# Start of a fused sparse-attention and MoE kernel: one load on another queue, mask copies dealt out anew, one subtraction on another engine

## The chip, the cores and the metric

One core of one Trainium2 chip runs the whole program. The time is device microseconds of one execution, and each kernel is given by the median of several runs. A profiled execution gives the trace; its span goes from the first to the last instruction, and the execution around it is a little longer.

## What is computed

Block-sparse attention over 4 batches of 8 heads (768 positions, 64 channels), and a two-layer feed-forward network on its output. Everything is float32 and has to come out at nearly float32 accuracy.

```python
scores = scale * np.matmul(q, k.transpose(0, 1, 3, 2))
mask = np.abs(blk_i - blk_j) <= window            # blocks of 32 positions, window 1
mask = mask | (blk_i == 0) | (blk_j == 0) | (blk_i == n_blocks - 1) | (blk_j == n_blocks - 1)
for qb in range(n_blocks):
    for kb in sampled_blocks[qb]:                 # 3 sampled blocks for each block row
        mask[qb * block:(qb + 1) * block, kb * block:(kb + 1) * block] = True
scores = np.where(mask, scores, -1000000000.0)
attn = np.exp(scores - np.max(scores, axis=-1, keepdims=True))
attn = attn / (np.sum(attn, axis=-1, keepdims=True) + 1e-09)
out = np.matmul(attn, v)
# then: h = x @ w_in; g = piecewise(h); return g @ w_out
```

## The kernel before

A float32 product is made of float32r products. A value is split into a high part (its value rounded to float32r) and a low part (the value less the high part). For a head, `load_qk` (L214) brings 64 rows of q and 64 rows of k, transposed, into one 128x768 tile `qk`; `hi` (L218, recorded at the helper's L196) rounds it on ScalarE into `qkh`; `lo` (L228) subtracts, on VectorE, and leaves the low part in the tile `qk`. Transfers from SBUF to SBUF then deal the rows out: `hi_one` (L224, L225) writes `KA` and `QA`, `hi_two` (L233, L234) writes the high halves of `QB` and `KB`, and `lo_two` (L237, L238) their low halves. They all go through SyncE's queue (SP), as nearly every transfer of the kernel does.

`KA` and `QA` are 128-row operands in which the rows above 64 carry the mask. Rows 64 and up of `KA` hold indicator rows (which block a column belongs to) and a row of ones for each query tile; rows 64 to 87 of `QA` hold the mask's penalties, and rows 96 and up the negated row maxima. So one matmul gives masked scores. There are two sets of these operands (`SETS = 2`): even heads use `QA[0]` and `KA[0]`, odd heads `QA[1]` and `KA[1]`.

The first computation of a head is twelve matmuls `max_mm` (L267), high part only, each followed by a maximum on VectorE (`max_red`, L272). The maxima are turned by a transpose with the identity `idr` (L280) and written to `QA` (L283). Then come the scores (L303 with `KA` and `QA`, L304 with `KB` and `QB`), the exponentials on ScalarE (L308) and the product with v (L333). Heads 0 to 9 use a simpler product with v. Beside the heads, the weights arrive as 64-bit numbers and are turned into float32 high and low parts (`convert`, L157 to L184: ScalarE L168, VectorE L169 to L174, ScalarE L196, GpSimd L180), and the two layers of the network follow batch by batch (L457 to L459, L485 to L487).

`consts` (L87 to L124) prepares the masks once. It loads the sampled blocks, a table, the indicator rows `ind` (38 rows of 768 numbers, into a borrowed buffer `raw`, L100) and the identity (L102). VectorE rounds the identity into `idr` (L103) and the indicator rows into `KA[0]` (L104); GpSimd rounds them into `KA[1]` (L108, recorded at L194). VectorE builds a 24x24 penalty table `mb`. For each half of the columns (384 of them) one matmul (L122) multiplies it with the indicator rows of `KA[0]` into one bank of PSUM, and the result is copied into rows 64 to 87 of both sets of `QA` (L124): set 0 by VectorE, set 1 by ScalarE.

The steps are put into a list with a planned time each and sorted by it; the plan of `consts` is at -90, the first `load_qk` at -99, the other steps of head 0 between -13 and 0. The framework's scheduler takes that order as a priority and not as a fixed order: on each engine it puts what it thinks is ready first. The order in the trace is the one that it made. It also gives the transfers from SyncE's and ScalarE's queues eight completion semaphores, in turn.

Of the kernel before, what the change touches and what calls it, by code (L numbers as in the profile page):

```python
# [10 lines left out]
I32 = mybir.dt.int32  # L11
U32 = mybir.dt.uint32
AF = mybir.ActivationFunctionType
ALU = mybir.AluOpType
# [4 lines left out]
B, H, S, D = 4, 8, 768, 64  # L19
NB, BLK, NR = 24, 32, 3  # L20
T = 6
HALF = 384
# [5 lines left out]
KM = 64 + NB  # L28
KA = 96 + T
# [8 lines left out]
def body(ctx, tc, qk_t, v, sampled_blocks, moe_w_in, moe_w_out, ind, cm, negd, ident, fold, out):  # L38
    nc = tc.nc
# [11 lines left out]
    op = pool("op", 1)  # L51
    wst = pool("wst", 3)
    cv = pool("cv", 1)
# [19 lines left out]
    def f(ap):  # L73
        return ap.bitcast(F32)


    idr = cst.tile([128, 128], F32R, name="idr")
# [4 lines left out]
    QA = [cst.tile([128, S], F32R, name=f"QA{i}") for i in range(SETS)]  # L82
# [4 lines left out]
    def consts():  # L87
        M = slice(64, KM)
        for i in range(SETS):
            nc.gpsimd.memset(f(QA[i][64:128 if i == 0 else 96]), 0.0)  # L90
        nc.gpsimd.memset(VW[0][:, :, 64:128], 1.0)
        nc.gpsimd.memset(VW[1][:, :, 0:64], 1.0)
        nc.vector.memset(eps, 1e-9)
        nc.vector.memset(half_c, 0.5)
        sraw = cst.tile([128, NR, 2], I32, name="sraw")
        nc.sync.dma_start(out=sraw[M], in_=sampled_blocks.bitcast(I32).rearrange("a (r w) -> a r w", w=2))
        cmt = cst.tile([128, 2 * NB], F32, name="cmt")
        nc.sync.dma_start(out=cmt[M], in_=cm)
        ef = f(cv.tile([128, 512, 2], I32, name="raw", bufs=3).rearrange("p c w -> p (c w)"))[64:KA, 0:S]
        nc.sync.dma_start(out=ef, in_=ind)  # L100
        idf = pp.tile([128, HALF], F32, name="pt")[:, 0:128]
        nc.sync.dma_start(out=idf, in_=ident)  # L102
        nc.vector.tensor_copy(out=idr, in_=idf)  # L103
        nc.vector.tensor_copy(out=KAt[0][64:KA], in_=ef)  # L104
        nc.sync.dma_start(out=nd, in_=negd.rearrange("a (t p) -> a t p", t=T))
        nc.sync.dma_start(out=sel, in_=fold)
        for i in range(1, SETS):
            rounded(nc.gpsimd, KAt[i][64:KA], ef)  # L108
        sf = cst.tile([128, NR], F32, name="sf")
        nc.vector.tensor_copy(out=sf[M], in_=sraw[M, :, 0])  # L110
        al = cst.tile([128, NB], F32, name="al")
        nc.vector.tensor_copy(out=al[M], in_=cmt[M, 0:NB])
        for r in range(NR):
            nc.vector.scalar_tensor_tensor(
                out=al[M], in0=cmt[M, NB:2 * NB], scalar=sf[M, r:r + 1], in1=al[M],
                op0=ALU.is_equal, op1=ALU.max)
        mb = cst.tile([128, NB], F32R, name="mb")
        nc.vector.tensor_scalar(out=mb[M], in0=al[M], scalar1=-1.0, scalar2=BIG, op0=ALU.add, op1=ALU.mult)
        for hf in range(2):
            cs = slice(hf * HALF, (hf + 1) * HALF)  # L120
            pm = psa.tile([128, 512], F32, name="pa")
            nc.tensor.matmul(out=pm[0:NB, 0:HALF], lhsT=mb[M], rhs=KAt[0][64:KM, cs], start=True, stop=True)  # L122
            for i in range(SETS):
                (nc.scalar.copy if i else nc.vector.tensor_copy)(out=QA[i][64:KM, cs], in_=pm[0:NB, 0:HALF])  # L124


    plan = []
# [62 lines left out]
    def rounded(eng, dst, src):  # L190
        if eng is nc.vector:
            eng.tensor_copy(out=dst, in_=src)
        elif eng is nc.gpsimd:
            eng.tensor_scalar(out=dst, in0=src, scalar1=1.0, scalar2=0.0, op0=ALU.mult, op1=ALU.add)  # L194
        else:
            eng.copy(out=dst, in_=src)  # L196

    def head(i, n0, b, h, pst):
# [7 lines left out]
        st = {}  # L206
# [18 lines left out]
            move(QAi[0:64], st["hi"][L])  # L225

        def lo():
            nc.vector.tensor_tensor(out=st["x"], in0=st["x"], in1=f(st["hi"]), op=ALU.subtract)  # L228

        def hi_two():  # L230
            st["KB"] = qk.tile([128, S], F32R, name="KB")
# [8 lines left out]
        def split(pl, n, src, hi, lo):  # L240
            t = st[n] = pl.tile([128, T, 128], F32R, name="vn")
            rounded(nc.scalar, t[:, :, hi], st[src])
            nc.gpsimd.tensor_tensor(out=t[:, :, lo], in0=st[src], in1=f(t[:, :, hi]), op=ALU.subtract)
# [12 lines left out]
        at(pre - G["qs"] - 0.4, hi)  # L256
        at(pre - G["qs"] + 0.2, hi_one)
        at(pre - G["qs"] + 0.4, lo)
        at(pre - G["qs"] + 1.3, hi_two)
        at(pre - G["qs"] + 1.6, lo_two)  # L260
# [21 lines left out]
        def max_row(lo=0, n=T):  # L282
            nc.vector.tensor_tensor(out=QAi[96:96 + n].rearrange("a (t p) -> a t p", t=T)[:, lo:n],  # L283
                                    in0=st["pr"][0:n, 0:128].unsqueeze(1).to_broadcast([n, n - lo, 128]),
                                    in1=nd[0:n, lo:n], op=ALU.mult)
# [240 lines left out]


    at(TC, consts)
    for i in range(NHEADS):
        b, h = divmod(i, H)  # L530
# [4 lines left out]
    p = PER * H / (2 * NF)  # L535
# [3 lines left out]
    for fq in range(4):  # L539
        for kt in range(4):  # L540
            cs = slice(fq * 512, (fq + 1) * 512)
# [86 lines left out]
```

## Time and profile before

| | us |
|---|---|
| median of 3 runs | 993.7 |
| the runs | 993.34, 993.7, 997.28 |
| the profiled execution | 991.61 |
| its span | 989.8 |
| busy in it: TensorE matmuls | 947.2 (96%) |
| VectorE | 735.9 (74%) |
| ScalarE | 637.2 (64%) |
| GpSimd | 323.5 (33%) |

PE is TensorE, PEld its weight loads, DVE VectorE, ACT ScalarE, POOL GpSimd, SP SyncE. A "q" behind an engine's name (SPq) means its sequencer, which issues transfers. In a timeline the first two columns are the start and the time, in us; behind a row stands the idle time of the engine before it and what ended it. A busy PE is not PE at its peak, since matmuls overlap: in a packed stretch they follow one another sooner than each one's own time.

### The profile page before, as it was taken

The page shows a single profiled execution, that of the slowest core. Times are in us where ns is not written, and L with a number is a line of the kernel's source. Part 1 is how long each engine was busy: PE and PEld are TensorE (multiplying, and loading weights), DVE is VectorE, ACT ScalarE, POOL GpSimd, SP SyncE. Part 2 cuts the span into 40 slices and gives each one's busy share as a digit, 9 for nine tenths or more (in the row PEclk, how much of TensorE's full clock was granted, in tenths as well). Part 3 has the DMA queues.
Part 4 walks back from the last instruction along what each step waited for, and adds up shares of the span by engine and source line. Part 5 has one row for each costly group of instructions (what it writes and reads, how often), then busy time and mean ns, then how long its engine had stood idle before and what let it go on. Part 6 is the DMA issues. An engine that isn't in the chain of part 4 may idle for free.

```text
span 989.8 us, 14583 instructions
## 1 busy us (share of the span) xinstructions
PE 947.2 (96%) x4687; PEld 830.4 (84%) x4687; DVE 735.9 (74%) x1349; ACT 637.2 (64%) x1302; POOL 323.5 (33%) x283
## 2 busy tenths in 40 slices
PE   5898899999899999999999999999999999999998
PEld 3666567778779989999989999998999899899996
DVE  5888887679998887888888897888888885422222
ACT  3676666666667666777767676866777676533433
POOL 1222120225554344444544444344544444000000
PEclk9999999999999999999999999999999999999999
DMA  6666676753455454656455454655546442434442
GB/s 196 200 182 184 190 207 204 228 180 103 155 170 172 128 141 129 186 151 174 136 143 175 133 150 137 184 158 152 156 130 187 116 124 86 154 128 128 160 128 96
DMA packets 56216, 154.43 MB, mean 156 GB/s; under 512 B 9612, under 2 KB 17952, under 8 KB 56140
## 3 DMA queue, kind: packets, MB, share of 16 engines
q1 hardware_dynamic: 56100, 153.48, 52.1%
q8 instruction: 37, 0.61, 0.3%
q14 instruction: 39, 0.32, 0.1%
q10 hardware_dynamic: 40, 0.03, 0.0%
HBM read 100.92 MB, written 14.81 MB: 117 GB/s over the span
## 4 chain that ended last, share of the span: by engine, by line
PE 70%; DVE 7%; ACT 2%; issue 1%; POOL 0%; POOLq 0%; ACTq 0%; DVEq 0%
PE oa L485 8%; PE oa L487 8%; PE oa L486 8%; PE hp L457 7%; PE hp L458 7%; PE hp L459 7%; PE po L335 5%; PE pa L303 4%; PE pa L304 4%; PE po L336 4%; PE pa L267 4%; DVE pl L316 2%; DVE mc L272 1%; PE pa L459 1%; PE pa L458 1%
## 5 line engine op out<-in xcount | busy, mean ns | idle before, releaser
L323 POOL TENSOR_TENSOR acc<-acc,pt 128x384 f32<-128x384 f32 x176 | 206.6, 1174 | 189.9 <-ACT pt L308 146.2
L272 DVE TENSOR_REDUCE mc<-pa 128x1 f32<-128x384 f32 x384 | 203.3, 549 | 20.4 <-PE pa L267 17.1
L196 ACT CAST ph<-pt 128x384 fp32r<-128x384 f32 x264 | 135.8, 514 | 94.4 <-PE po L335 90.1
L316 DVE TENSOR_TENSOR pl<-pt,ph 128x384 fp32r<-128x384 f32 x264 | 166.9, 632 | 33.3 <-ACT ph L196 32.4
L308 ACT ACTIVATE pt<-pa 128x384 f32<-128x384 f32 x288 | 140.5, 489 | 49.6 <-PE pa L304 41.6
L457 PE MATMUL hp<-x,wi 128*128 128x384 f32 x448 | 156.3, 349 | 5.4 <-DVE r L469 5.3
L485 PE MATMUL oa<-w,gh 128*128 128x512 f32 x384 | 153.3, 399 | 0.3 <-ACT gh L196 0.3
L459 PE MATMUL hp<-x,wi 128*128 128x384 f32 x448 | 152.1, 340 | 0.0
L458 PE MATMUL hp<-x,wi 128*128 128x384 f32 x448 | 152.0, 339 | 0.0
L487 PE MATMUL oa<-w,gl 128*128 128x512 f32 x384 | 151.5, 394 | 0.0
L486 PE MATMUL oa<-w,gh 128*128 128x512 f32 x384 | 150.8, 393 | 0.0
L267 PE MATMUL pa<-KA,QA 88*128 88x384 f32 x384 | 139.4, 382 | 8.8 <-DMA QA<-qkh 5.9
L469 DVE SCALAR_TENSOR_TENSOR r<-r,hp 128x384 f32<-128x384 f32 x112 | 61.8, 552 | 74.6 <-ACT r L466 74.4
L478 DVE TENSOR_TENSOR gl<-r,gh 128x384 fp32r<-128x384 f32 x128 | 91.0, 711 | 30.2 <-ACT gh L196 28.1
L267 PEld LDWEIGHTS pa<-KA,QA 88*128 88x128 f32 x384 | 73.4, 193 | 33.2 <-DVE mc L272 11.2
L303 PE MATMUL pa<-QA,KA 102*128 102x384 f32 x288 | 99.7, 346 | 0.7 <-DVE mc L272 0.4
L463 ACT ACTIVATE r<-hp,half_c 128x384 f32<-128x384 f32 x112 | 65.1, 581 | 52.3 <-PE hp L459 49.2
L304 PE MATMUL pa<-QB,KB 128*128 128x384 f32 x288 | 98.3, 341 | 0.0
L335 PE MATMUL po<-ph,vn 128*128 128x384 f32 x264 | 91.9, 348 | 4.7 <-DVE xun L345 3.9
L457 PEld LDWEIGHTS hp<-x,wi 128*128 128x128 f32 x448 | 85.0, 190 | 12.3 <-DVE r L469 7.8
L323 POOL TENSOR_TENSOR acc<-pt 128x384 f32<-128x384 f32 x44 | 45.6, 1037 | 136.7 <-ACT pt L308 132.9
L336 PE MATMUL po<-pl,vn 128*128 128x384 f32 x264 | 88.8, 336 | 0.0
(97 smaller groups left out, 1665.7 us busy)
## 6 DMA issues: line engine op xcount, KB each, us to landing
w<-wo_dram SPq DMA_DIRECT2D x112, 512.0 KB
qk<-in_qk_t_dram SPq DMA_DIRECT2D x32, 384.0 KB
raw<-in_moe_w_in_dram SPq DMA_DIRECT2D x16, 512.0 KB
raw<-in_moe_w_out_dram SPq DMA_DIRECT2D x16, 512.0 KB
wo_dram<-w SPq DMA_DIRECT2D x16, 512.0 KB
lv<-in_v_dram SPq DMA_DIRECT2D x32, 192.0 KB
KA<-qkh SPq DMA_DIRECT2D x32, 192.0 KB
QA<-qkh SPq DMA_DIRECT2D x32, 192.0 KB
```

The costliest lines, as they stand in the source:

```text
L267: nc.tensor.matmul(out=pm[:, 0:HALF], lhsT=QAi[0:KM, t * 128:(t + 1) * 128], rhs=KAi[0:KM, kh * HALF:(kh + 1) * HALF], start=True, stop=True)
L272: nc.vector.reduce_max(out=st["mc"][:, t, kh:kh + 1], in_=st.pop(("pm", t, kh))[:, 0:HALF], axis=AX.X)
L308: nc.scalar.activation(out=p, in_=st.pop(("ps", c))[:, 0:HALF], func=AF.Exp, scale=SCALE)
L316: (nc.gpsimd if i < 2 * H and c in PL1 else nc.vector).tensor_tensor(out=pl, in0=st["p", c], in1=f(st["ph", c]), op=ALU.subtract)
L323: nc.gpsimd.tensor_tensor(out=st["acc", hf], in0=prev, in1=st["p", c], op=ALU.add)
L335: nc.tensor.matmul(out=po, lhsT=st["vn"][:, c], rhs=st["ph", c], start=(c == 0), stop=False)
L457: nc.tensor.matmul(out=hv, lhsT=wi[:, j, 0, fs], rhs=x[:, 0], start=(j == 0), stop=False)
L458: nc.tensor.matmul(out=hv, lhsT=wi[:, j, 0, fs], rhs=x[:, 1], start=False, stop=False)
L459: nc.tensor.matmul(out=hv, lhsT=wi[:, j, 1, fs], rhs=x[:, 0], start=False, stop=(j == NP - 1))
L485: nc.tensor.matmul(out=o, lhsT=gh[:, ts], rhs=w[:, 0], start=(fi == 0), stop=False)
L486: nc.tensor.matmul(out=o, lhsT=gh[:, ts], rhs=w[:, 1], start=False, stop=False)
L487: nc.tensor.matmul(out=o, lhsT=gl[:, ts], rhs=w[:, 0], start=False, stop=(fi == NF - 1))
```

## The change

Three edits in `consts` and one in `head`. The load of the indicator rows is issued from ScalarE's queue, and written ahead of the other loads of `consts`. The identity is rounded by ScalarE, as the last statement of `consts`, instead of by VectorE. The copies of the mask rows are dealt out by half instead of by set: VectorE copies the first half of the columns into both sets, ScalarE the second half. And `lo` of head 0 (`i` is the number of the head) is done by GpSimd instead of VectorE; every other head keeps it on VectorE.

```diff
         nc.vector.memset(half_c, 0.5)
+        ef = f(cv.tile([128, 512, 2], I32, name="raw", bufs=3).rearrange("p c w -> p (c w)"))[64:KA, 0:S]
+        nc.scalar.dma_start(out=ef, in_=ind)
         sraw = cst.tile([128, NR, 2], I32, name="sraw")
         nc.sync.dma_start(out=sraw[M], in_=sampled_blocks.bitcast(I32).rearrange("a (r w) -> a r w", w=2))
         cmt = cst.tile([128, 2 * NB], F32, name="cmt")
         nc.sync.dma_start(out=cmt[M], in_=cm)
-        ef = f(cv.tile([128, 512, 2], I32, name="raw", bufs=3).rearrange("p c w -> p (c w)"))[64:KA, 0:S]
-        nc.sync.dma_start(out=ef, in_=ind)
         idf = pp.tile([128, HALF], F32, name="pt")[:, 0:128]
         nc.sync.dma_start(out=idf, in_=ident)
-        nc.vector.tensor_copy(out=idr, in_=idf)
         nc.vector.tensor_copy(out=KAt[0][64:KA], in_=ef)
...
             for i in range(SETS):
-                (nc.scalar.copy if i else nc.vector.tensor_copy)(out=QA[i][64:KM, cs], in_=pm[0:NB, 0:HALF])
+                (nc.scalar.copy if hf else nc.vector.tensor_copy)(out=QA[i][64:KM, cs], in_=pm[0:NB, 0:HALF])
+        nc.scalar.copy(out=idr, in_=idf)
...
         def lo():
-            nc.vector.tensor_tensor(out=st["x"], in0=st["x"], in1=f(st["hi"]), op=ALU.subtract)
+            (nc.vector if i else nc.gpsimd).tensor_tensor(out=st["x"], in0=st["x"], in1=f(st["hi"]), op=ALU.subtract)
```

## Rows read from the trace of the kernel before

**Rows 1.** The page: the busy time of each engine, and PE's busy share in 40 equal slices of the span (a digit is a slice's share in tenths).

```profile
PE 947.2 (96%) x4687; PEld 830.4 (84%) x4687; DVE 735.9 (74%) x1349; ACT 637.2 (64%) x1302; POOL 323.5 (33%) x283
...
PE   5898899999899999999999999999999999999998
```

**Rows 2.** Busy time of the engines by stretch (the stretch, its length, then PE, PEld, DVE, ACT, POOL in us with the count of instructions, the granted clock, the DMA share and GB/s).

```profile
0.00:25.00 25.00, 13.55 (x41) 9.75 (x42) 14.47 (x35) 9.23 (x17) 3.50 (x9) 1.00 0.68 196
25.00:50.00 25.00, 22.38 (x89) 16.57 (x88) 22.06 (x42) 15.72 (x32) 6.24 (x4) 0.93 0.67 197
50.00:100.00 50.00, 45.27 (x186) 32.08 (x184) 43.41 (x82) 35.80 (x73) 10.45 (x8) 1.00 0.68 186
100.00:150.00 50.00, 43.67 (x173) 29.88 (x172) 43.97 (x84) 33.88 (x69) 9.53 (x7) 1.00 0.69 199
150.00:200.00 50.00, 49.17 (x223) 39.03 (x223) 34.88 (x67) 30.55 (x61) 6.13 (x5) 1.00 0.67 212
200.00:250.00 50.00, 46.19 (x217) 39.34 (x216) 40.95 (x70) 33.58 (x68) 19.40 (x16) 0.97 0.45 136
250.00:300.00 50.00, 45.25 (x217) 38.37 (x216) 48.47 (x81) 33.55 (x72) 27.06 (x22) 0.97 0.51 163
...
600.00:800.00 200.00, 198.72 (x1047) 182.89 (x1048) 167.24 (x306) 142.21 (x296) 89.27 (x80) 1.00 0.53 154
```

**Rows 3.** The timeline of the first 20 us, all engines and the queues (rows between them left out).

```profile
0.74 1.28 ACT L196 ACT_TABLE_LOAD   x1 [0.74 <-PEq L608]
0.74 0.40 SPq L214 DMA_DIRECT2D qk<-in_qk_t_dram  x1
...
2.02 0.26 SPq L100 DMA_DIRECT2D raw<-in_ind_dram  x1
...
4.03 0.83 ACT L196 CAST qkh<-qk 128x768 fp32r<-128x768 f32 x1 [2.00 <-DMA qk<-in_qk_t_dram]
...
4.88 0.53 SPq L221 DMA_DIRECT2D KA<-qkh  x1
...
5.46 0.59 SPq L221 DMA_DIRECT2D QA<-qkh  x1
...
7.61 0.46 SPq L221 DMA_DIRECT2D KB<-qkh  x1
7.61 0.56 DVE L104 CAST KA<-raw 38x768 fp32r<-38x768 f32 x1 [2.35 <-DMA raw<-in_ind_dram]
7.76 1.10 POOL L194 TENSOR_SCALAR KA<-raw 38x768 fp32r<-38x768 f32 x1 [4.78 <-DMA raw<-in_ind_dram]
8.20 1.47 DVE L228 TENSOR_TENSOR qk<-qk,qkh 128x768 f32<-128x768 f32 x1
...
8.23 0.83 PE L122 MATMUL pa<-KA,mb 24*24 24x384 f32 x2 [8.23 <-DVE KA L104]
9.59 0.21 DVE L103 CAST idr<-pt 128x128 fp32r<-128x128 f32 x1
...
9.84 1.01 DVE L124 CAST QA<-pa 24x384 fp32r<-24x384 f32 x2
10.20 0.60 SPq L238 DMA_DIRECT2D KB<-qk  x1
10.48 0.87 ACT L124 CAST QA<-pa 24x384 fp32r<-24x384 f32 x2 [5.62 <-DVE QA L124]
...
11.36 2.93 PE L267 MATMUL pa<-KA,QA 88*128 88x384 f32 x6 [2.31 <-DMA QA<-qkh]
...
13.76 0.33 SPq L214 DMA_DIRECT2D qk<-in_qk_t_dram  x1
...
15.19 0.27 PE L280 MATMUL pa<-idr,mr 128*3 128x128 f32 x1 [0.90 <-DVE mr L276]
...
16.91 0.52 PE L304 MATMUL oa<-QB,KB 128*128 128x384 f32 x1
...
19.77 0.66 ACT L168 ACTIVATE cva<-raw 128x512 f32<-128x512 f32 x1
```

**Rows 4.** What SyncE's queue waited for in the first 30 us, and the transfer that TensorE's first score matmul waited for in the same stretch (us in total, times, longest).

```profile
SPq L214 <- DMA KB<-qk: 1.0, 1, 1.0
...
SPq L221 <- DMA raw<-in_ind_dram: 0.9, 1, 0.9
...
PE pa L267 <- DMA QA<-qkh: 2.3, 1, 2.3
```

**Rows 5.** Half-microsecond stretches of the start, columns as in rows 2; the last two are the busy share of the 16 DMA engines and GB/s.

```profile
2.50:3.00 0.50, 0.00 (x0) 0.00 (x0) 0.00 (x0) 0.00 (x0) 0.49 (x2) 1.00 0.85 338
...
5.50:6.00 0.50, 0.00 (x0) 0.00 (x0) 0.00 (x0) 0.00 (x0) 0.00 (x0) 1.00 0.18 65
...
9.00:9.50 0.50, 0.06 (x1) 0.00 (x0) 0.50 (x1) 0.00 (x0) 0.00 (x0) 1.00 0.98 209
...
10.00:10.50 0.50, 0.00 (x0) 0.00 (x0) 0.50 (x2) 0.02 (x1) 0.00 (x0) 1.00 0.14 31
```

**Rows 6.** GpSimd's groups of subtractions and additions by shape (count, then busy us and mean ns, then the idle time before them), and all of VectorE's `lo` (shortest, median and longest ns, first and last start).

```profile
L323 POOL TENSOR_TENSOR acc<-pt 128x384 f32<-128x384 f32 x44 | 45.6, 1037 | 136.7 <-ACT pt L308 132.9 <-DVE psum L358 3.8
...
L180 POOL TENSOR_TENSOR w<-cva,w 128x512 fp32r<-128x512 f32 x16 | 22.7, 1420 | 74.8 <-DVE gl L478 37.3 <-ACT w L196 32.8 <-DMA QA<-qkh 4.7
...
L228 DVE TENSOR_TENSOR qk<-qk,qkh x32: 893/946/1466, 8.2 to 779.5; 128x768 f32<-128x768 f32 x32
```

## The prediction

> **What bounds the kernel now.** I read the page first: TensorE is busy for 947.2 of 989.8 us, and the only slice far below the others is the first, at five tenths [rows 1]. The change touches nothing but that slice, so I then read the busy time by stretch: the first 25 us hold 13.55 us of matmuls; later stretches are packed to 99% (198.72 of 200) or, between 25 and 300 us, to 87 to 98%, with VectorE at 70 to 97% beside them [rows 2]. The reader is to see that there is no second place where the edits act directly: what they can give is the time by which the first score matmul starts earlier, passed on to a kernel that is mostly TensorE from then on.
>
> Next the timeline of the start, read backwards from that matmul. L267 starts at 11.36, and what released it is the transfer into `QA` [rows 3, 4]. That transfer was issued at 5.46, so it took 5.9 us [rows 3]. The mask path, which the change mostly rebuilds, was done a little earlier: indicator rows landed by 7.61, `KA` copy to 8.17, mask matmuls to 9.06, then VectorE did `lo` (8.20 to 9.67) and `idr` before it got to its mask copies at 9.84, which ended at 10.85 [rows 3]. So there are two paths into the first matmul, and the mask copies of set 0 are the second to last, half a microsecond ahead of `QA`. Ending that path earlier gives nothing unless `QA` also lands earlier.
>
> Why is `QA` so slow? While it is still under way, at 10.0 to 10.5, the DMA engines are busy for 0.14, some two of sixteen; at 9.0 to 9.5 they were at 0.98 [rows 5]. The same picture stands at 5.5 to 6.0 (0.18, 65 GB/s), when the indicator rows are what is outstanding [rows 3, 5]. I read this as two engines that carry the whole of `ind` and fall behind with their shares of everything queued after it, `KA` and `QA` among them.
>
> **The load of the indicator rows.** Before, it is the fourth transfer on SyncE's queue, issued at 2.02 and landed at 7.61: 5.6 us [rows 3]. ScalarE issues nothing in this stretch. An issue there costs between 0.26 and 0.60, as SyncE's do, and with the table load of 1.28 it ends long before `qk` releases ScalarE at 4.03 (idle 2.00 before it) [rows 3], so the issue itself is hidden. Issued at 0.74 with the same 5.6 us, `ind` lands at 6.3. The bounds: as quick as `qk` on all engines, 3.3 us, gives 4.0; if the table load goes first on ScalarE, it is issued near 2.0 and lands at 7.6, as now [rows 3]. I take 6.3, since the row is the same transfer. In return `qk` may be later: at 338 GB/s [rows 5] one of 16 engines moves 21 GB/s, its share of the 384 KB is 24 KB or 1.1 us, and if it alternates with `ind` on two engines, `qk` lands up to 1.1 us later.
>
> **The wait that comes with it.** The issue of `KB` at 7.61 waited for `ind`, though it doesn't read it [rows 3, 4]. Transfers take eight completion semaphores in turn: `ind` was the fourth and `KB` the twelfth. With `ind` moved to first or second place, its follower eight places on is `KA` or `QA`. So one of the two now waits for `ind` to land. Behind the waiting issue stand, in SyncE's queue, the other moves, `lo_two`, the next v, the first raw weights and the next `qk`. `QA` is issued at 6.4 if it is the one that waits, or at 6.9 behind `KA`, whose issue takes 0.53 [rows 3], instead of 5.46. A delay of `hi` by 1.1 us (end at 6.0, `KA` at 6.05) is covered by that wait to within 0.3 us.
>
> How long does `QA` take then? With `ind` landed, the two engines are free of it. The nearest row without that backlog is `KB<-qk`, issued at 10.20 and landed when it releases the next `qk` at 13.76: 3.56 us [rows 3, 4]. That gives 9.96 or 10.5; the middle is 10.2, **1.2 us earlier** than 11.36. The bounds: `ind` at 4.0 leaves `QA` at its old 5.46 and 9.0, so -2.3; the old 5.9 us from the new issue gives 12.3 or 12.8, so +0.9 to +1.4. I stay near the first price, because the tail at two engines [rows 5] is gone once `ind` is through.
>
> **The mask path** after: `ind` at 6.3, `KA` copy 0.56, mask matmuls 0.83, then two copies on each engine side by side, 1.01 on VectorE and 0.87 on ScalarE [rows 3]: 8.7. Before, ScalarE's copies of a half waited for VectorE's of the same half; that wait goes. The path is 1.5 us ahead of `QA` and gives nothing by itself; if that cover went, it would still allow 8.7.
>
> **`idr` on ScalarE**: one small copy, 0.21 on VectorE [rows 3], up to the 0.44 of a mask copy on ScalarE. Its reader is the transpose at 15.19, some 4 us later even after a shift of 1.2. Nothing.
>
> **`lo` on GpSimd.** GpSimd takes 1037 ns for 384 columns and 1420 for 512 [rows 6], so 2.1 us for 768, against 1.47 here and 0.95 usually on VectorE [rows 6]. It needs `hi` and, if the scheduler keeps the written order, stands behind GpSimd's `KA[1]` copy of 1.10, which waits for `ind`: 6.3 + 1.1 + 2.1 = 9.5, against 9.67 before. With `ind` at 7.6 it is 10.8. Its moves feed L304 at 16.91, and the second one landed at 13.76: 3.1 us of cover. The raw weights behind them in SyncE's queue are first read at 19.77 [rows 3]. Nothing, up to a delay of 3 us.
>
> **The sum**: -1.2 us at the first matmul. The maxima, the transpose and the first scores hang on it step by step [rows 3], so I carry the whole of it to the end: 989.8 becomes 988.6, and 991.61 becomes 990.4. The profiled execution lies 2.1 below the median of 993.7, and two of three runs are within 0.4 of that, so I subtract from the median: **992.5**.
>
> **The rivals.** *The two engines stay the last.* Both queues may be served by the same engines, so the two slow ones carry the same bytes before `QA`'s, whatever the queue; `QA` lands at 11.3 as now. For it: the tail of two engines is what ends last [rows 5]. Against it: `ind` is issued 1.3 us sooner (0.74 for 2.02), and if the two engines start on it sooner, they are through with the list sooner. The time is 993.7. The Trainium skill (DMA: Bandwidth & Descriptors, section Issuing engines are not separate DMA queues) states just this: transfers from several engines interleave on the same 16 DMA engines, and another issuing engine saves only the time to issue. By that rule the gain is near nothing; no row of this stretch has two queues at work, so the trace can't decide it.
>
> *`QA` hangs on `ind`* and loses. The place is the semaphore wait on SyncE; the price is the new issue time plus the old 5.9 us, +0.9 to +1.4, so 994.9. It decides against the change from the point at which `ind` lands later than 7.7, or 7.2 with `KA` in front (11.36 less 3.56, less the issue). For it: the wait is seen today on `KB` [rows 4]; against it: `ind` must become slower than it is.
>
> *The scheduler's order changes further on.* The trace shows that it doesn't keep the written order: L103 runs after L228, which is written much later [rows 3]. A start with other times can turn pairs on VectorE and ScalarE for a long stretch. What that can move is TensorE's idle time from 25 to 300 us: 2.6 + 4.7 + 6.3 + 0.8 + 3.8 + 4.8 = 23 us [rows 2]. A quarter of it either way is 6 us: 988 or 999.
>
> **How the numbers follow.** Chances: the forecast 0.50, the two engines 0.15, the semaphore 0.13, another order 0.22, half to each side, of which 0.09 and 0.11 reach beyond 0.5%. That is 5.0 us, about what a measurement of this kernel can tell from no change; its own runs spread over 4. So faster 0.09, same 0.80, slower 0.11. The range takes in -2.3, +1.4, the spread of the runs above the median (997.28), and the smaller part of the reorderings: 988.8 to 997.5.
>
> **What would show it.** Right: L267 starts near 10.2, released by a transfer into `QA` or `KA`; SyncE waits for `ind` at `KA` or `QA` and no longer at `KB`; the two-engine tail before L267 is gone. Wrong: L267 still at 11.3 (two engines), later than 11.4 (semaphore), or a start that moved while TensorE's busy share between 25 and 300 us changed by more than the shift (order). A mask copy as the releaser of L267 would show that I priced the `QA` transfer too high.

## The result, and the profile after

The changed kernel took 998.87 us (median of 8 runs, 997.85 to 1002.19) beside 993.03 for the kernel before (8 runs, 989.69 to 997.28): a ratio of 1.0063, with an interval of 1.0043 to 1.0083. It is slower, by some 6 us, where the prediction said 1.2 us faster; the time lies above its range.

The page of the changed kernel, as [rows 1]: the same work, more idle time, and the first slice down from five tenths to three.

```profile
span 997.4 us, 14588 instructions
...
PE 950.7 (95%) x4687; PEld 832.6 (83%) x4687; DVE 735.3 (74%) x1347; ACT 637.6 (64%) x1303; POOL 325.1 (33%) x284
...
PE   3898889998899999999999999999999999999998
```

Busy time by stretch, as [rows 2]. TensorE does 9.89 us of matmuls in the first 25, where it did 13.55, a lack of 3.7, and another 1.0 less in the next 25. Between 600 and 800 it is as packed as before (199.03 of 200 us).

```profile
0.00:25.00 25.00, 9.89 (x28) 7.31 (x29) 14.53 (x32) 8.38 (x15) 6.59 (x11) 1.00 0.72 194
25.00:50.00 25.00, 21.38 (x75) 14.81 (x74) 22.93 (x39) 15.77 (x32) 5.73 (x5) 0.86 0.68 188
...
600.00:800.00 200.00, 199.03 (x1047) 183.19 (x1047) 166.01 (x305) 142.43 (x297) 87.44 (x78) 1.00 0.52 153
```

The timeline of its start, as [rows 3] (line numbers from L96 to L123 are one or two off those of before).

```profile
0.74 0.55 ACTq L96 DMA_DIRECT2D raw<-in_ind_dram  x1
0.74 0.39 SPq L214 DMA_DIRECT2D qk<-in_qk_t_dram  x1
...
5.91 0.83 ACT L196 CAST qkh<-qk 128x768 fp32r<-128x768 f32 x1 [3.31 <-DMA qk<-in_qk_t_dram]
6.61 0.33 SPq L162 DMA_DIRECT2D raw<-in_moe_w_in_dram  x1
6.62 0.56 DVE L103 CAST KA<-raw 38x768 fp32r<-38x768 f32 x1 [5.72 <-DMA raw<-in_ind_dram]
...
7.05 0.53 SPq L221 DMA_DIRECT2D KA<-qkh  x1
...
7.63 0.59 SPq L221 DMA_DIRECT2D QA<-qkh  x1
...
7.95 1.80 POOL L228 TENSOR_TENSOR qk<-qk,qkh 128x768 f32<-128x768 f32 x1
7.99 2.34 DVE L113 SCALAR_TENSOR_TENSOR al<-cmt,sf,al 24x24 f32<-24x24 f32 x3
...
10.59 0.83 PE L121 MATMUL pa<-KA,mb 24*24 24x384 f32 x2 [10.59 <-DVE mb L117]
...
11.21 1.01 DVE L123 CAST QA<-pa 24x384 fp32r<-24x384 f32 x2 [0.68 <-PE pa L121]
...
13.94 0.43 DVE L170 TENSOR_SCALAR cva<-cva 128x512 int32<-128x512 int32 x1
...
14.14 1.30 PE L267 MATMUL pa<-KA,QA 88*128 88x384 f32 x3 [2.72 <-DMA QA<-qkh]
14.40 0.69 DVE L172 SCALAR_TENSOR_TENSOR cva<-raw,cva 128x512 int32<-128x512 int32 x1
15.13 0.69 DVE L174 SCALAR_TENSOR_TENSOR cva<-raw,cva 128x512 int32<-128x512 int32 x1
15.74 2.87 DVE L272 TENSOR_REDUCE mc<-pa 128x1 f32<-128x384 f32 x6
...
18.86 0.27 PE L280 MATMUL pa<-idr,mr 128*3 128x128 f32 x1 [0.90 <-DVE mr L276]
```

Four things are to be seen. The indicator rows came 1.0 us earlier (6.62 for 7.61), but q and k 1.9 later (5.91 for 4.03). In SyncE's queue a load of 512 KB of raw weights now stands ahead of `KA` and `QA`; before, the first such load was issued after all of head 0's moves. `QA` was issued at 7.63 and releases L267 at 14.14: 6.5 us, beside 5.9 before. The traces also hold the times at which a transfer's completion semaphore rose, sixteen times for `QA`: before, fourteen of these rises had come by 9.14 and the last two came at 10.90 and 11.23, the tail that the prediction put down to two engines; here all sixteen came between 11.95 and 14.00. That tail is gone, and the whole of `QA` is late. And when the first score matmul was done, VectorE was busy with the weights' conversion (L170 to L174), so the first maximum (L272) waited until 15.74. The first transpose (L280), which was at 15.19, is at 18.86: the start is 3.7 us late.

What SyncE's queue waited for in the first 20 us (us in total, times, longest): the weight load, not `KA` or `QA`, is now the transfer eight places behind `ind`.

```profile
SPq L162 <- DMA raw<-in_ind_dram: 2.9, 1, 2.9
```

### The profile page after: what moved, and what is told of

It reads as the page before. It is cut to its first block, busy times and chain, and to the rows that moved or that the text cites. A ratio compares the mean times of both kernels' runs of the same rounds, so it can differ in the third digit from the quotient of the medians.

```text
span 997.4 us, 14588 instructions
## 1 busy us (share of the span) xinstructions
PE 950.7 (95%) x4687; PEld 832.6 (83%) x4687; DVE 735.3 (74%) x1347; ACT 637.6 (64%) x1303; POOL 325.1 (33%) x284
## 4 chain that ended last, share of the span: by engine, by line
PE 78%; DVE 12%; ACT 3%; issue 3%; DMA 3%; POOL 1%; SPq 0%; ACTq 0%; DVEq 0%; POOLq 0%
PE oa L485 8%; PE oa L487 8%; PE oa L486 8%; PE hp L457 7%; PE hp L459 7%; PE hp L458 7%; PE pa L267 6%; PE po L335 5%; PE pa L303 5%; PE pa L304 4%; PE po L336 4%; DVE mc L272 3%; PE po L333 3%; PE oa L333 2%; DVE pl L316 2%
## 5 line engine op out<-in xcount | busy, mean ns | idle before, releaser
L272 DVE TENSOR_REDUCE mc<-pa 128x1 f32<-128x384 f32 x384 | 203.2, 548 | 24.3 <-PE pa L267 21.2
L267 PE MATMUL pa<-KA,QA 88*128 88x384 f32 x384 | 139.4, 382 | 9.1 <-DVE mc L272 4.5
L267 PEld LDWEIGHTS pa<-KA,QA 88*128 88x128 f32 x384 | 73.9, 194 | 32.6 <-DVE mc L272 12.1
L304 PE MATMUL pa<-QB,KB 128*128 128x384 f32 x288 | 98.1, 340 | 0.0
```

Source lines behind the costliest of these rows:

```text
L267: nc.tensor.matmul(out=pm[:, 0:HALF], lhsT=QAi[0:KM, t * 128:(t + 1) * 128], rhs=KAi[0:KM, kh * HALF:(kh + 1) * HALF], start=True, stop=True)
L272: nc.vector.reduce_max(out=st["mc"][:, t, kh:kh + 1], in_=st.pop(("pm", t, kh))[:, 0:HALF], axis=AX.X)
```

## The experiments

The column "L280" is the start of the first transpose in the profiled execution (15.19 before; the line is L283 in the kernels with added lines); it tells how late the start is. All times are medians beside runs of the kernel before on the same chip (993.03 for the changed kernel, 992.91 for the next four rows, 992.2 for the four after them, 993.63 for the last three). The ratio and its interval are an estimate of their own and not the quotient of the two medians (e_hold: 1.0023, where the medians give 1.0005).

| run | L280, us | shift | median, us | ratio to before (interval) |
|---|---|---|---|---|
| the changed kernel | 18.86 | +3.67 | 998.87 | 1.0063 (1.0043 to 1.0083) |
| e_queue | 18.39 | +3.20 | 1000.57 | 1.0083 (1.0055 to 1.0111) |
| e_noqueue | 14.90 | -0.29 | 993.95 | 1.0012 (0.9993 to 1.0031) |
| e_spread | 12.61 | -2.58 | 988.83 | 0.9957 (0.9938 to 0.9976) |
| e_aspread | 17.47 | +2.28 | 996.73 | 1.0046 (1.0028 to 1.0064) |
| e_hold | 15.51 | +0.32 | 992.7 | 1.0023 (1.0004 to 1.0043) |
| e_hold_nolo | 14.44 | -0.75 | 989.88 | 0.9979 (0.9958 to 0.9999) |
| e_slow | 16.40 | +1.21 | 991.46 | 0.9996 (0.9979 to 1.0014) |
| e_spread_nq | 13.47 | -1.72 | 989.2 | 0.9977 (0.9959 to 0.9994) |
| e_wfirst | 18.93 | +3.74 | 1000.33 | 1.0061 (1.0037 to 1.0085) |
| e_mended | 13.60 | -1.59 | 990.16 | 0.9961 (0.9945 to 0.9978) |
| e_spread_copies | 12.58 | -2.61 | 991.05 | 0.9971 (0.9949 to 0.9994) |

### Which of the edits

e_queue is the kernel before with the first edit alone; e_noqueue is the changed kernel without it.

```diff
 # e_queue, against the kernel before
+        ef = ... [64:KA, 0:S]
+        nc.scalar.dma_start(out=ef, in_=ind)
         sraw = cst.tile([128, NR, 2], I32, name="sraw")
...
-        nc.sync.dma_start(out=ef, in_=ind)
 # e_noqueue, against the changed kernel: the same lines the other way round
```

> The kernel before with one edit alone: the indicator rows issued from ScalarE's queue, ahead of the other loads. Theory Q (the queue edit is the whole loss): like the changed kernel, 5 to 6.5 us over before; SyncE sends the first raw weights ahead of KA and QA, head 0's q and k land near 5.9 instead of 4.0, the first score matmul L267 starts at 13.5 to 14.2. Rival G (the subtraction on GpSimd is the loss, since it triples VectorE's three small steps on the penalty table and delays the mask matmul from 8.2 to 10.6): within 1 us of before.

> The changed kernel with the indicator rows back on SyncE's queue in their old place; the mask copies by half, the identity on ScalarE and the subtraction on GpSimd stay. Theory Q: within 1 us of before (-1 to +0.5), L267 at 11.3 since QA still lands there, the mask copies end near 9.3 to 10. Rival G: 4 to 6 us over before.

Theory Q held in both: the queue edit alone gives the whole loss, and without it the time is that of before within the interval. The sizes are off (7.7 us between the medians for a forecast of 5 to 6.5, and 1.0 for at most 0.5). The other edits are not the cause. The mask copies by half did what they should (in e_noqueue L267 was released by `QA` at 11.07, 0.9 us after the last mask copy), and it bought nothing, as forecast. In e_queue the whole order of TensorE's work is that of the changed kernel, and SyncE sends the weights first (6.52, then `KA` at 6.96); in e_noqueue the orders of TensorE and SyncE are those of before. So the order of the work follows the queue edit.

### Is the weight load the cause, or ScalarE's queue?

e_hold keeps all of the change and holds back the first two weight loads; e_wfirst keeps the kernel before and sends the first weight load early.

```diff
 # e_hold, against the changed kernel, in convert's load()
             st["raw"] = cv.tile([128, 512, 2], I32, name="raw", bufs=3)
+            loads.append(1)
+            if len(loads) <= 2:
+                nc.gpsimd.tensor_copy(out=f(st["raw"])[0:64, 0, 0:1], in_=f(QA[0])[0:64, 0:1])
 # e_wfirst, against the kernel before, in plan_conversions(); n counts the conversions from the last planned
-            at(t - P["cl"], load)
+            at(-12.6 if n == len(conv) - 1 else t - P["cl"], load)
```

> The changed kernel, in which the first two loads of raw weights wait until QA of head 0 has landed (GpSimd copies one column of QA into each raw tile before its load; the tile is then overwritten). Theory W (the weight load that SyncE sends ahead of KA and QA, and the conversion steps that then stand ahead of the maxima, are half of the late start): QA lands near 11 instead of 14, L267 starts at 11 to 12.5, the first column of maxima is 0.5 to 1.5 us later than before instead of 3.7, and the end 1 to 2 us over before. Rival O (the new order further on costs by itself): the first maxima as said, but the end still 3 us or more over before.

> The kernel before with one thing changed: the first load of raw weights is planned right after head 0's rounding, so that SyncE sends it ahead of KA and QA. The indicator rows stay on SyncE, the mask copies, the identity and the subtraction stay as before. From there on every engine's order is that of the changed kernel. Theory W (that weight load is the cause, by its traffic ahead of QA and its conversion steps ahead of the maxima): L267 at 13 to 14.5, the first maxima 3 to 4 us late, the end 4.5 to 6.5 us over before, as in the changed kernel. Rival Q2 (ScalarE's queue itself is the cause, since q and k come 1.9 us later there): less than 3 us over before.

The timeline of e_wfirst. `ind` is on SyncE's queue as before, q and k land as early as before, the mask copies end at 11.3, and still L267 starts at 14.28 behind `QA`, which was issued at 5.30.

```profile
3.87 0.83 ACT L196 CAST qkh<-qk 128x768 fp32r<-128x768 f32 x1 [1.85 <-DMA qk<-in_qk_t_dram]
3.95 0.42 SPq L162 DMA_DIRECT2D raw<-in_moe_w_in_dram  x1
...
5.30 0.59 SPq L221 DMA_DIRECT2D QA<-qkh  x1
...
10.28 1.01 DVE L124 CAST QA<-pa 24x384 fp32r<-24x384 f32 x2
...
14.28 1.30 PE L267 MATMUL pa<-KA,QA 88*128 88x384 f32 x3 [4.78 <-DMA QA<-qkh]
```

Theory W held from both sides. With the loads held back, the change costs 0.3 us at the start and 1.0023 (0.4 to 4.3 us by the interval, 0.5 between the medians); with nothing but the early weight load, the kernel before is as slow as the changed one (1.0061 beside 1.0063) and late by the same 3.7 us. That q and k land 1.9 us later on account of ScalarE's queue is real, and alone it costs little: e_hold has it too (rounding at 5.80). There `QA` was issued at 7.24 and had landed by 10.40, when GpSimd's copy of its column starts: 3.2 us, and earlier than in the kernel before. The mask copies were the last into the first score matmul.

```profile
7.24 0.59 SPq L224 DMA_DIRECT2D QA<-qkh  x1
...
10.40 0.30 POOL L164 COPY raw<-QA 64x1 f32<-64x1 f32 x2 [0.80 <-DMA QA<-qkh]
...
11.66 2.96 PE L270 MATMUL pa<-KA,QA 88*128 88x384 f32 x6 [0.40 <-DVE QA L123]
```

The two runs don't weigh the same. Holding the loads also gave TensorE an order of its own: it differs from that of before up to matmul 483 and from that of the changed kernel up to 617, so e_hold is not the changed kernel less one transfer. In e_queue and e_wfirst TensorE's order is that of the changed kernel in all 4687 matmuls, and these two carry the argument. What the changed order costs further on, apart from the load's traffic, no run separates.

Why the load came forward was not tried; it was read from the program. The scheduler fills a queue with whatever it thinks ready. Before, SyncE still had loads to issue when it took head 0's rounding to be done; with one load fewer there was a gap, and the next ready transfer, planned much later, went into it.

### Two DMA engines

e_spread and e_slow are the kernel before with the indicator rows in two transfers; the order of work on every engine is that of before, but for one pair: VectorE does head 0's subtraction ahead of the `KA` copy and not behind it. e_aspread is the changed kernel with 32 and 6 rows.

```diff
-        nc.sync.dma_start(out=ef, in_=ind)
 # e_spread (e_aspread: the same on nc.scalar)
+        [nc.sync.dma_start(out=ef[r0:r1], in_=ind[r0:r1]) for r0, r1 in ((0, 32), (32, 38))]
 # e_slow
+        [nc.sync.dma_start(out=ef[r0:r1], in_=ind[r0:r1]) for r0, r1 in ((0, 37), (37, 38))]
```

> The kernel before with the indicator rows loaded by two transfers on SyncE's queue, of 32 and 6 rows, instead of one of 38; every engine's order of work is that of before. If one transfer of 38 rows is carried by two DMA engines and these hold up QA (the reading of the prediction), QA lands near 9, the indicator rows near 5, L267 starts at 9 to 10, and the end is 1.5 to 2.3 us earlier, at about 991. If the late landing of QA has another cause, L267 stays at 11.3 and the time is that of before.

> The kernel before with the indicator rows loaded by two transfers of 37 and 1 rows on SyncE's queue; every engine's order is that of before. If the number of DMA engines follows from the number of rows, one engine now carries 37 rows, the indicator rows land some 2 to 3 us later than at 7.6, and L267 starts at 13.5 to 15. It is a late start with nothing else changed. Theory S (a late start is carried to the end as it is): the end moves by the shift of the first maxima, 2 to 3.5 us. Rival A (a late start grows on the way): by 1.4 times the shift or more, 3.5 to 5 us. Rival D (it is made up later): by less than half of it.

> The changed kernel with the indicator rows loaded by two transfers of 32 and 6 rows on ScalarE's queue; every engine's order of work is that of the changed kernel. q and k should land near 4.0 again instead of 5.9. Theory S (the loss is the late start, carried to the end): L267 1.9 to 4 us earlier than in the changed kernel and the end earlier by as much, so 0 to 3 us over before. Rival O (the new order of VectorE's and ScalarE's work after the start costs some 3 to 4 us by itself): the start is mended but 3 us or more over before remain, more than the shift of the first maxima.

e_spread: the rows are there at 5.17 instead of 7.61, `QA`, issued at 5.44 as before, no longer holds up TensorE, and the mask copies release L267 at 8.74.

```profile
2.01 0.70 SPq L100 DMA_DIRECT2D raw<-in_ind_dram  x2
...
5.17 0.83 POOL L194 TENSOR_SCALAR KA<-raw 38x768 fp32r<-38x768 f32 x1 [2.19 <-DMA raw<-in_ind_dram]
...
5.44 0.59 SPq L221 DMA_DIRECT2D QA<-qkh  x1
...
8.74 2.97 PE L267 MATMUL pa<-KA,QA 88*128 88x384 f32 x6 [0.47 <-DVE QA L124]
```

e_slow: they are there at 10.34.

```profile
10.34 0.56 DVE L104 CAST KA<-raw 38x768 fp32r<-38x768 f32 x1 [4.21 <-DMA raw<-in_ind_dram]
...
12.57 2.92 PE L267 MATMUL pa<-KA,QA 88*128 88x384 f32 x6 [0.79 <-DMA QA<-qkh]
```

The same bytes take 8.3 us, 5.6 us or 3.2 us from issue to use when cut as 37 and 1, as 38, or as 32 and 6 rows. The Trainium skill (DMA: Bandwidth & Descriptors, section on why a DMA increments its semaphore by 16 and not by 1) says that a transfer is spread over the largest number up to 16 that divides its slowest dimensions: two engines for 38 rows, sixteen for 32, one for 37. The three durations agree in their order, and so do the rises of the semaphores: without one rise close to the issue, there is one for 37 rows (10.06), two for 38 (7.15 and 7.59), sixteen for 32 and six for 6.

e_spread has the lowest median and ratio of the study. Its start is 2.6 us earlier, its median 4.1; the interval (2.4 to 6.2 us) takes in the 2.6. e_slow didn't come out as forecast: L267 at 12.57 instead of 13.5 to 15, a start only 1.2 us late (fifteen rises of `QA`'s semaphore by 8.44, the last at 12.44), and no loss at the end (0.9996, interval -2.1 to +1.4 us). It speaks against growth of a late start (rival A), and can't tell full carrying from a loss made up. e_aspread has the changed order with q and k less late (rounding at 4.59): the start is 1.4 us earlier than in the changed kernel and the median 2.1. That lies between the two theories as they were put; 3.8 us over before against a shift of 2.3 is more than the start explains.

### GpSimd's subtraction, and the parts together

e_hold_nolo is e_hold with head 0's subtraction on VectorE; e_mended is that with the rows in 32 and 6 on ScalarE's queue; e_spread_nq is e_noqueue, and e_spread_copies the kernel before with the mask copies by half and the identity on ScalarE, both with 32 and 6 rows on SyncE's queue.

```diff
 # e_hold_nolo, against e_hold
-            (nc.vector if i else nc.gpsimd).tensor_tensor(out=st["x"], ...)
+            nc.vector.tensor_tensor(out=st["x"], ...)
```

> The same as the run with the held weight loads, with the subtraction of head 0 back on VectorE. If GpSimd's subtraction holds up VectorE's three small steps on the penalty table, these take 0.8 us in all instead of 2.3, the mask matmul starts near 9 instead of 10.6, and L267 is released by QA's landing near 11 rather than by the mask copies near 12.3: up to 1.2 us earlier at the first maxima. If the two engines don't hold each other up, the mask matmul starts at the same time in both.

> The run with held weight loads and the subtraction on VectorE, in which the indicator rows, still on ScalarE's queue, come by two transfers of 32 and 6 rows. q and k land near 4.5 instead of 5.7, the indicator rows near 5.2 instead of 6.6. If these late landings are what still bounds its start (L270 at 10.6 there), the first score matmul starts at 8.7 to 9.5 and the time falls by 1 to 2 us, to about 988.5. If not, it stays at 989.9.

> The changed kernel with the indicator rows back on SyncE's queue and loaded by two transfers of 32 and 6 rows; the mask copies by half, the identity on ScalarE and the subtraction on GpSimd stay. In the run with two transfers alone the mask copies released L267, behind the subtraction on VectorE; with that on GpSimd they end near 7.5 and QA is next, near 8.4. Forecast: L267 at 8.3 to 8.6 instead of 8.74, so the time of that run or up to 0.5 us less, about 988.5. If these parts cost something of their own, the time is above that run by 1 us or more.

> The kernel before with the indicator rows by two transfers of 32 and 6 rows on SyncE's queue, and with the mask copies by half and the identity on ScalarE; the subtraction stays on VectorE. In the run with two transfers alone L267 started at 8.74, released by VectorE's mask copies. With the copies side by side it starts at 8.5 to 8.7, so the time is that of that run within 0.3 us, near 988.8 beside 992.9. If the copies by half cost something, it is above by 1 us or more.

The same stretch of e_hold:

```profile
7.80 1.80 POOL L231 TENSOR_TENSOR qk<-qk,qkh 128x768 f32<-128x768 f32 x1
7.84 2.33 DVE L113 SCALAR_TENSOR_TENSOR al<-cmt,sf,al 24x24 f32<-24x24 f32 x3
...
10.43 0.83 PE L121 MATMUL pa<-KA,mb 24*24 24x384 f32 x2 [10.43 <-DVE mb L117]
```

and of e_hold_nolo, where nothing runs on GpSimd beside the three steps:

```profile
6.75 1.11 POOL L197 TENSOR_SCALAR KA<-raw 38x768 fp32r<-38x768 f32 x1 [3.76 <-DMA raw<-in_ind_dram]
...
7.08 0.80 DVE L109 CAST sf<-sraw 24x3 f32<-24x3 int32 x1
...
7.98 0.77 DVE L113 SCALAR_TENSOR_TENSOR al<-cmt,sf,al 24x24 f32<-24x24 f32 x3
...
9.02 0.83 PE L121 MATMUL pa<-KA,mb 24*24 24x384 f32 x2 [9.02 <-DVE mb L117]
```

GpSimd's subtraction makes three steps of 0.77 us take 2.33, and the mask matmul 1.4 us later. In e_hold the mask path was the last into the first score matmul, so this counts: without it the transpose comes 1.07 us earlier, as forecast (though the mask copies, at 10.59, and not `QA` are still the last), and the median is 2.8 lower. TensorE's order differs between the two runs as well, up to matmul 628, so what the subtraction costs beyond the 1.07 us isn't shown. In the changed kernel it was hidden behind `QA`. The 32 and 6 rows on top (e_mended) brought the start another 0.84 forward (first score matmul 9.74, a little later than the 8.7 to 9.5 forecast); beside their own runs of before the two ratios, 0.9979 and 0.9961, overlap. e_spread_nq missed its forecast at the start: GpSimd's subtraction again slowed VectorE's small steps (2.35 us for the three) and L267 came at 9.62, later than e_spread's 8.74. e_spread_copies started nearly as forecast, at 8.72. None of the four came below e_spread (0.9957), and none is told apart from it: their intervals overlap.

## Why the prediction was wrong, step by step

**What bounds the start** was right: two engines behind the rows (the last two rises of `QA`'s semaphore), `QA` last into L267, the mask path next. e_spread, which mends just that, gained 0.43% with TensorE's order of before.

**`ind` on ScalarE's queue**: landing forecast at 6.3, seen at 6.6. q and k up to 1.1 us later: seen 1.9. Fourteen rises of their semaphore had come by 3.96, the last two came at 5.71 and 5.89: two engines had to do both transfers. The Trainium skill (DMA: Bandwidth & Descriptors, section Issuing engines are not separate DMA queues) says that transfers from several engines interleave on the same DMA engines, and these rows agree; the prediction had quoted it for a rival.

**The wait** is the step that failed. It counted eight places on from `ind` in the queue of before and found `KA` or `QA`; the eight places were right, but the follower is a weight load that wasn't there before. The prediction listed that load behind `QA`, as in the old order, and priced `QA` from 7 us on as having the engines to itself (3.56 us). With 512 KB ahead of it, `QA` took 6.5 us, and was issued at 7.6 instead of 6.4 to 6.9, in part since q and k were late (e_hold, without the load, issued it at 7.2): 14.1 instead of 10.2. The price itself was good: in e_hold `QA` took 3.2 us and had landed by 10.4. e_wfirst shows that the early load, with the order that follows from it, makes the loss. The semaphore rival's sign, a start later than 11.4, was there without its cause: SyncE's wait for `ind` ended at 6.61, before `hi` did at 6.74, so `KA` and `QA` lost at most 0.3 us by it.

**The order** was a rival, with 0.22, but it was priced as chance, a quarter of TensorE's idle time from 25 to 300 us either way. It had a definite place: the gap in the queue that the edit itself made. That its upper value, 999, is close to the measured 998.87 is luck: TensorE's busy time from 25 to 300 us, where it was priced, changed by only 0.7 us (251.9 to 251.3), and the lack is in the first 25. The order also decides the second loss at the start: VectorE's conversion steps stand ahead of the first maxima and hold them up by 0.9 us (14.14 and 0.7 for a matmul against 15.74).

**The sum carried to the end**: the lateness at L280 is 3.67, the loss 5.8 between the medians. The kernels with the changed order (the changed kernel, e_queue, e_wfirst, e_aspread) lose 1.5 to 4.5 us more between the medians than their L280 is late; among the others the difference lies between -2.0 and +1.3 us. Part of it can be seen. Between the maxima of head 0 and those of head 1 VectorE does two conversions and most of a third in the changed kernel; in the kernel before it did two. Head 1's twelve maxima begin at 33.34 instead of 28.74, and the step behind them (L276) at 39.71 instead of 34.99.

```profile
31.82 0.42 DVE L169 TENSOR_SCALAR cva<-cva 128x512 f32<-128x512 f32 x1
32.27 0.43 DVE L170 TENSOR_SCALAR cva<-cva 128x512 int32<-128x512 int32 x1
32.73 0.69 DVE L172 SCALAR_TENSOR_TENSOR cva<-raw,cva 128x512 int32<-128x512 int32 x1
33.34 5.86 DVE L272 TENSOR_REDUCE mc<-pa 128x1 f32<-128x384 f32 x12
...
39.71 0.16 DVE L276 TENSOR_TENSOR mr<-mc 128x6 fp32r<-128x6 f32 x1
```

The kernel before:

```profile
28.74 6.00 DVE L272 TENSOR_REDUCE mc<-pa 128x1 f32<-128x384 f32 x12 [0.39 <-PE pa L267]
...
34.99 0.16 DVE L276 TENSOR_TENSOR mr<-mc 128x6 fp32r<-128x6 f32 x1
```

So 3.7 us have become 4.7 there. At the same step e_queue is 4.6 us late, e_wfirst 5.9 and e_aspread 3.2; the medians lose 1.1 us more than that in the changed kernel, 3.1 in e_queue, 0.8 in e_wfirst and 0.6 in e_aspread. e_queue's runs had a mean granted clock of 0.9895, those of before beside them 0.9928, which by the fit below is worth 2.0 of its 3.1. So all but about a microsecond of the loss stands by 40 us. Where that microsecond is added is open.

**The mask path**: forecast to end at 8.7, it ended near 12.2. VectorE took the `KA` copy first, then the small steps, and these were stretched by GpSimd. I had priced GpSimd's `lo` at 2.1 us (seen: 1.80) and its effect on VectorE at nothing. Hidden behind `QA` here, it showed in e_hold. GpSimd was done with `lo` at 9.75, forecast at 9.5, and the second of its moves had landed by 17.66, ahead of the first L304 at 20.57.

**`idr` on ScalarE** was not tried alone; e_noqueue and e_spread_copies have it, and no loss shows in them, as forecast.

## What to carry to other kernels

Where a scheduler orders the work by readiness, taking a transfer out of a queue is not the removal of one item: ask which later transfer will fill the gap, how large it is, and what stands behind it. A transfer that few engines carry (two, by its semaphore, for the 38 rows here) holds up their shares of everything queued after it; cut it (38 into 32 and 6) before moving it to another queue. A step moved to GpSimd is not free for VectorE even if VectorE doesn't wait for its result.

## What was not expected of the hardware

**GpSimd beside VectorE.** Three VectorE steps on 24x24 numbers, 0.77 us alone, took 2.33 us while GpSimd subtracted 128x768 numbers in 1.80: the first of the three took 1.80 and ended 0.03 us after the subtraction, the others took 0.23 each. The Trainium skill (GPSIMD Engine Reference, section Key points) says that GpSimd shares its SBUF interfaces with VectorE, and that they contend where VectorE's instruction has two SBUF inputs or runs in a 2-port mode; these steps have two inputs, and the rows agree. A cast with one input (L109, 0.16 us in e_noqueue) was held as well: it took 0.80 in the changed kernel, e_hold and e_hold_nolo, and ended with GpSimd's copy into `KA[1]`.

**The clock.** In the changed kernel, TensorE was busy for 1.46 of 4.00 us, and then the granted clock stood at 0.50, 1.2 of 2.4 GHz, for 6.8 us; in the profile of before there is such a stretch a little earlier, about half as long. Columns as in rows 2; the last two lines are the kernel before.

```profile
37.00:41.00 4.00, 1.46 (x6) 0.65 (x4) 3.97 (x9) 2.64 (x5) 0.48 (x1) 1.00 0.23 61
41.00:47.80 6.80, 6.40 (x15) 4.68 (x16) 6.36 (x9) 4.71 (x9) 2.07 (x2) 0.50 0.69 194
...
35.00:38.20 3.20, 1.81 (x9) 1.47 (x10) 3.13 (x8) 1.77 (x5) 0.00 (x0) 1.00 0.59 155
38.30:41.50 3.20, 3.20 (x8) 2.05 (x7) 2.42 (x4) 1.84 (x4) 1.34 (x1) 0.50 0.91 232
```

The runs of one kernel differ in it: the changed kernel took 997.85 us at a mean granted clock of 0.995 and 1002.19 at 0.987. A line fitted to the 217 runs with a clock on record, within each kernel, gives 0.6 us more for every 0.001 less of mean granted clock and takes up 45% of the spread. So single profiles mislead: the changed kernel's, 4.7 us late at 39.71, is 6.1 late behind the slow stretch (L276 at 57.14 for 51.02) and 7.7 behind the next one (92.05 for 84.36), where the medians differ by 5.8. But the clock is not the loss: e_wfirst's runs had a mean of 0.9931, those of before beside them 0.9925, and their median is 6.7 us higher.
